# Column tiles for the values of two more pairs of head groups, and other ranks for four streams of a planned kernel

## The chip, the cores and the metric

The kernel runs on one core of a Trainium2 chip. The metric is the device time of one execution in microseconds. A core has a matmul engine (PE, with its weight loads listed as PEld), a vector engine (DVE), a scalar engine (ACT), GpSimd (POOL) and SyncE (SP), whose queue issues nearly all DMAs here.

## The reference

Two layers over a sequence of 2048 tokens of width 640, each an attention block and a feed-forward block, with layer norm ahead of each and a residual sum behind it. All weights are shared by the two layers.

```python
for layer in range(2):
    x = x + attention(layernorm(x), wq, wk, wv, wo, beta)
    h = layernorm(x)
    x = x + max(h @ w1, 0) @ w2            # w1: 640 x 1728

# attention: 32 heads of 20, four segments of 512 tokens; g = sigmoid(beta), per head
for s in range(4):
    p = softmax(q_s k_s^T / sqrt(20), causal inside the segment)
    a_dot = p v_s
    a_mem = phi(q_s) M / (phi(q_s) z + 1e-6)   # phi(t) = t + 1 if t > 0 else exp(t)
    o_s = g * a_mem + (1 - g) * a_dot
    M, z = M + phi(k_s)^T v_s, z + sum phi(k_s)
return concat(o) @ wo
```

## The kernel before

The program is not written as loops. Every piece of the work is a Python generator, called a stream, which yields operations (an engine, an assumed duration, the instructions, what they wait for) and requests for buffers and events. A planner, `Sched.run`, takes one operation after the other and so writes out each engine's order of instructions ahead of time. It picks the operation that can start first by its own reckoning; among those that start at the same nanosecond, the lower rank wins. The rank is the first argument of `S.add(rank, stream)` at the end of `plan`. Streams of rank 0, the score products and the exponentials, may also keep an engine from starting something that would delay them.

```python
key = (round(start + late), op.urgent * 0.5 if op.urgent else prio, n)
```

The kernel makes a whole plan for each value in `STARTS`, which is the price in ns that the planner puts on a change of PE's tile mode, and keeps the plan that comes out shortest by its own reckoning with random lateness of DMAs (`late`). PE works in three modes: `full` (the 128 x 128 array), `rows` (four row tiles, for the scores, whose contraction is a head of 20) and `cols` (column tiles). An operation in column mode that is ready while PE is in full mode is held up to 4 us (`JOIN_NS`), so that it can follow a round of scores. Where the planner sees no work for PE it puts in idle matmuls on a unit matrix (`keep_busy`, line 627).

A segment's 32 heads are 8 groups of 4, taken as 4 pairs; `m` counts the pairs over both layers, 0 to 31, and pairs 0 to 3 are the first segment of the first layer. For each pair the steps are:

- `fill` brings q and k of the pair's heads into a padded buffer, by DMA from a scratch area in HBM that `spill` has written.
- `scores` (line 1103) and `exps` (L1155) run in five rounds over two halves of PSUM; `causal` (L1167) masks on POOL.
- `apply` multiplies the probabilities by the values. There are two forms. In the first segment of the first layer, `values_by_token` (L1197) has the probabilities stationary and 21 value columns moving, so that tokens come out on the partitions; DVE divides straight from PSUM (L1209 to L1213). Everywhere else the values are stationary in four column tiles (L1246); the result is copied out of PSUM (L1254 on DVE or L1255 on ACT), `turn_av` transposes it by a DMA through SP's queue, and `divide` (L1282 to L1290) divides it on DVE.
- `combine` adds the memory's part, `turn_o` transposes o by DMA, `out_proj` multiplies by wo and adds to x (L1317).

`phi_(0)` and `phi_(1)` compute phi of k and of q (L956 and L964 on DVE, L963 on ACT), `turn_k` transposes phi(k) by DMA, `mem_write` (L1047 to L1068) updates the memory and `mem_read(0)` and `mem_read(1)` (L996 to L1007) read it for one half of the heads each. `ffn` is the feed-forward; `ffn_last` (L1394) computes the last 64 of its 1728 hidden columns in two column tiles and is a stream of its own, whose result `ffn` waits for.

The planner streams run through all 8 pairs of layer and segment in order. Full-array products of the projections, of `out_proj` and of `ffn` come from one helper, with the first product of a group on line 640 and the others on line 643; all DMA transposes are issued on line 671.

Of the kernel before, what the change touches and what calls it, by code (L numbers as in the profile page):

```python
# [14 lines left out]
NSEG = 4  # L15
# [4 lines left out]
G = H // 4  # L20
# [137 lines left out]

LONE_NS = 300.0
SWITCH_NS = 97.0  # L160
STARTS = [SWITCH_NS + 0.75 * (k - 32 // 2) for k in range(32)]
LATE_NS = 300.0
JOIN_NS = 4000.0
SEM_NS = 60.0
# [212 lines left out]
def pe(ns, fns, waits=(), acq=None, take=(), mode="full"):  # L377
    return Op([("pe", ns, fns, 190.0)], waits, acq=acq, take=take, mode=mode)
# [6 lines left out]
def dve(n, mode, fn, waits=(), extra=0.0, acq=None, urgent=False):  # L385
    return Op([("dve", 66.0 + n / (0.96 * mode) + extra, [(fn, True)], 95.0)], waits, acq=acq, urgent=urgent)


def act(n, fn, waits=(), psum=True):
    return Op([("act", (52.0 if psum else 94.0) + n / 1.2, [(fn, True)], 125.0)], waits)  # L390
# [17 lines left out]
def plan(switch, sb, sem_, psum, dram, A_x, A_wq, A_wk, A_wv, A_wo, A_beta, B_x, B_w1, B_w2, out):  # L408
    P = Prog({e: sem_("clk_" + e) for e in ["act", "dve", "pool", "pe"]})
    S = Sched(P, switch)  # L410
# [437 lines left out]
    def sx(a, s):  # L848
        return 1 if (a, s) == (0, 1) else 0
# [92 lines left out]
    def phi_(n):  # L942
        def f(a, s):
            if s == (NSEG - 1, 0)[n]:
                for c in range(FC):
                    p = yield Need("packed", a, s, c)
                    STG[sx(a, s)][n][c].release(*p)
                return
            done = []
            for c in range(FC):  # L950
                if n == 0 and c in (0, 3):
                    yield Acq([PHS[c // 3]])
                raw = yield Need("stg", a, s, c, n)
                q = STGS[sx(a, s)][:, c, n, :]
                rt = yield Acq(RT)
                tr = yield dve(512, 4, lambda e, rt=rt, q=q: e.tensor_scalar(  # L956
                    rt.ap, q, 0.0, 1.0, ALU.max, ALU.add), raw + rt.tks)
                if n == 0:
                    dst, w = phs[:, c * L:(c + 1) * L], raw + PHS[c // 3].tks
                else:  # L960
                    p = yield Need("packed", a, s, c)
                    dst, w = q, [tr] + p
                te = yield act(512, lambda e, q=q, dst=dst: e.activation(dst, q, ACT.Exp), w, psum=False)  # L963
                tp = yield dve(512, 2, lambda e, rt=rt, dst=dst: e.tensor_tensor(dst, dst, rt.ap, ALU.min),  # L964
                               [te, tr])
                rt.release(tp)
                done.append(tp)
                if n == 0:
                    p = yield Need("packed", a, s, c)
                    STG[sx(a, s)][0][c].release(te, tr, *p)  # L970
                    if sx(a, s):
                        early_done.extend([te, tr] + p)
                    if c in (2, 4):
                        S.set("phk", a, s, c // 3, tks=done)
                        done = []
            if n == 1:
                S.set("phi", a, s, tks=done)
        return f
# [4 lines left out]
    def mem_read(hb):  # L983
        def f(a, s):
            if s == 0:
                return
            phi = yield Need("phi", a, s)
            bdt = yield Need("BD", a, s - 1)
            yield Acq([OMS[hb]])
            wr = []  # L990
            lst = [(c, max(CH_H0[c], 16 * hb), min(CH_H1[c], 16 * hb + 16)) for c in range(FC)]
            lst = [x for x in lst if x[1] < x[2]]
            for i in range(NJ):
                fns = []
                for z, (c, h0, h1) in enumerate(lst):
                    fns.append((lambda e, bk, c=c, h0=h0, h1=h1, z=z, i=i: e.matmul(  # L996
                        bk.ap[:, (h0 - 16 * hb) * 21:(h1 - 16 * hb) * 21],
                        STGS[sx(a, s)][:, c, 1, i * 128:(i + 1) * 128],
                        BD[:, CH_OFF[c] + (h0 - CH_H0[c]) * 21:CH_OFF[c] + (h1 - CH_H0[c]) * 21],
                        start=(z == 0), stop=True, skip_group_check=True), z == len(lst) - 1))  # L1000
                bk, tk = yield pe(60.0 * len(lst), fns, phi + bdt, acq=MISC[:1])
                rm = yield Acq(RMEM[hb])
                om = bk.ap[:, 0:336].rearrange("p (h e) -> p h e", e=21)
                ta = yield dve(16, 1, lambda e, rm=rm, om=om: e.tensor_scalar(
                    rm.ap, om[:, :, DH:DH + 1], 1e-6, None, ALU.add), [tk] + rm.tks)
                tr = yield dve(96, 1, lambda e, rm=rm: e.reciprocal(rm.ap, rm.ap), [ta])
                tm = yield dve(320, 1, lambda e, rm=rm, om=om, i=i: e.tensor_tensor(  # L1007
                    om_sb[:, i, 320 * hb:320 * hb + 320].rearrange("p (h e) -> p h e", e=DH),
                    om[:, :, 0:DH], rm.ap.to_broadcast([128, 16, DH]), ALU.mult), [tr] + OMS[hb].tks)
                rm.release(tm)  # L1010
                bk.release(tm)
                wr.append(tm)
            S.set("omem", a, s, hb, tks=wr)
            READ.setdefault((a, s), []).append(tk)
            if len(READ[a, s]) == 2:
                for c in range(FC):
                    STG[sx(a, s)][1][c].release(*READ[a, s])
                if sx(a, s):
                    S.set("q01", tks=READ[a, s])
                BDS.release(*READ[a, s])  # L1020
        return f
# [154 lines left out]

        return 32 if (g, hh) != (G - 1, 3) else DH + 1

    BY_TOKEN = ((0, 0),)

    def values_by_token(m, a, s, g0, vt):

# [37 lines left out]
    def done_values(a, s, g0, tk):  # L1220
        if g0 == G - 2:
            dmt = yield Need("dm", a, s)
            VA[vx(a, s)].release(tk, *dmt)
            if (a, s) == (0, 0):
                S.set("v00", tks=VA[3].tks)

    def apply(m):

        a, r = divmod(2 * m, NSEG * G)
        s, g0 = divmod(r, G)  # L1230
        vt = yield Need("v", a, s)
        if (a, s) in BY_TOKEN:
            tk = yield from values_by_token(m, a, s, g0, vt)
            yield from done_values(a, s, g0, tk)
            return
        sl = None
        ev = []
        for z in range(2):
            mk = yield Need("p", 2 * m + z)
            pt, mk = mk[0], mk[1:]  # L1240
            if sl is None:
                sl = yield Acq([AV])
            fns = []
            for j in range(NJ):
                for hh in range(4):
                    fns.append((lambda e, bk, j=j, hh=hh, pt=pt, g=g0 + z: e.matmul(  # L1246
                        bk.ap[32 * hh:32 * hh + wide(g, hh), 128 * j:L],
                        VAUG[vx(a, s)][:, j].rearrange("p h e -> p (h e)")[
                            :, (4 * g + hh) * (DH + 1):(4 * g + hh) * (DH + 1) + wide(g, hh)],
                        pt.ap[:, hh, PT_OFF[j]:PT_OFF[j] + L - 128 * j], start=(j == 0), stop=(j == NJ - 1)),  # L1250
                        j == NJ - 1 and hh == 3))
            bk, tk = yield pe(545.0, fns, mk + vt, acq=MISC, mode="cols")
            pt.release(tk)
            te = yield evac(L, 1, lambda e, sl=sl, z=z, bk=bk: e.tensor_copy(sl.ap[:, z], bk.ap),  # L1254
                            lambda e, sl=sl, z=z, bk=bk: e.activation(sl.ap[:, z], bk.ap, ACT.Copy), [tk] + sl.tks)  # L1255
            bk.release(te)
            ev.append(te)
        S.set("av", m, tks=[sl] + ev)
        yield from done_values(a, s, g0, tk)

    LATER = range(len(BY_TOKEN) * G // 2, NSEG * G)

    def turn_av(m):
        ev = yield Need("av", m)
# [207 lines left out]
    def each(f):  # L1472
        for a, s in AS:
            yield from f(a, s)
# [8 lines left out]
    S.add(1, items(apply, NSEG * G))  # L1483
    S.add(2, items(turn_av, LATER))
    S.add(6, items(divide, LATER))
    S.add(2, each(hot(turn_o)))
# [5 lines left out]
    S.add(5.5, each(spill))  # L1492
    S.add(2, each(combine))
    S.add(4, each(phi_(0)))
    S.add(4, each(phi_(1)))
    S.add(4, each(mem_read(0)))
    S.add(1, each(mem_read(1)))
    S.add(4, each(turn_k))
    S.add(4, each(mem_write))
    S.add(5, first_ln_a())  # L1500
    S.add(5, first_ln_b())
# [3 lines left out]
    S.add(5, each(proj_one(1)))  # L1505
    S.add(4, each(proj_v))
    S.add(6, each(ffn))
    S.add(6, each(ffn_last))
    S.add(7, warm_pe())
    S.add(3, consts())  # L1510
    S.add(8, loads())
# [6 lines left out]
def bass_interleave_layers__memory_aug_infini_attn__dense_activation_relu__prompt_kernel(  # L1518
    nc, A_x, A_wq, A_wk, A_wv, A_wo, A_beta, B_x, B_w1, B_w2, out,
):  # L1520
    with contextlib.ExitStack() as es:
# [10 lines left out]
        dram = lambda name, shape: once(name, lambda: nc.dram_tensor(name, shape, dt.bfloat16, kind="Internal").ap())  # L1532
        plans = [plan(k, sb, sem_, psum, dram, A_x, A_wq, A_wk, A_wv, A_wo, A_beta, B_x, B_w1, B_w2, out) for k in STARTS]
        S = min(plans, key=lambda p: sum(p.late(n) for n in range(4)))
# [31 lines left out]
```

## Time and profile before

| | |
|---|---|
| median of 3 runs | 566.28 us (564.82 to 566.39) |
| the profiled execution | 565.3 us, of which 563.5 are the span of instructions |
| PE, DVE, ACT, POOL busy | 99%, 75%, 72%, 35% of the span |
| L1197, values by token | 320 matmuls |
| L1246, values by column tiles | 896 matmuls |
| L627, idle matmuls | 66 |
| L1394, ffn_last | 80 matmuls |
| DMA, mean share of the 16 engines | 45.5% on the main queue |

The span is counted from the first to the last instruction; the profiled execution's own time has 1.8 us around it. In lists of groups a row gives line, engine, operation, output and inputs, the count, busy time and mean duration in ns, and then idle time of the engine before these instructions and what ended it. In timelines a row is start, length, engine, line and what is done, with the number of instructions merged. Matmuls overlap in the pipeline, so the distance between two starts is the time that one takes from PE's queue, and not its duration.

### The profile page before, as it was taken

What the parts mean: (1) busy time and instruction counts of PE and PEld (TensorE: products, weight loads), DVE (VectorE), ACT (ScalarE), POOL (GpSimd) and SP (SyncE); (2) the same over time, 40 slices, a digit from 0 to 9 for tenths busy, and PEclk for the clock granted to TensorE, in tenths of its full rate; (3) what the DMA queues carried; (4) which work ended last, traced back from release to release, by engine and by line L of the source; (5) the groups of instructions that cost most, each with busy time, mean ns of one, the idle gap of its engine ahead of it and who ended that gap; (6) DMA issues with size and microseconds to landing.
All of it is one profiled execution on the core that took longest, in us unless ns stands there. A gap on an engine that the chain in (4) does not pass through costs nothing.

```text
span 563.5 us, 12875 instructions
## 1 busy us (share of the span) xinstructions
PE 556.4 (99%) x5219; PEld 305.0 (54%) x5219; DVE 420.1 (75%) x1070; ACT 404.2 (72%) x512; POOL 195.1 (35%) x302
## 2 busy tenths in 40 slices
PE   8999999999999999999999999999999999999998
PEld 7664555445554454645446544555445654665655
DVE  6989789888999689878898997688747964560202
ACT  4789998987788878778986688778878678113140
POOL 4544344333344335444433443035322433110000
PEclk9999999999999999999999999999999999999999
DMA  8695988383474136542375131880326410512101
GB/s 268 120 221 138 238 218 182 74 224 56 97 171 94 44 88 159 118 95 72 92 163 115 27 66 26 193 148 20 67 80 173 109 43 20 116 45 48 47 1 47
DMA packets 130109, 60.93 MB, mean 108 GB/s; under 512 B 108930, under 2 KB 119938, under 8 KB 130050
## 3 DMA queue, kind: packets, MB, share of 16 engines
q1 hardware_dynamic: 129830, 59.85, 45.5%
q8 instruction: 41, 0.67, 0.5%
q10 hardware_dynamic: 220, 0.26, 0.2%
q14 instruction: 18, 0.15, 0.1%
HBM read 20.57 MB, written 12.85 MB: 59 GB/s over the span
## 4 chain that ended last, share of the span: by engine, by line
PE 87%; DVE 8%; DMA 2%; ACT 1%; SPq 1%; issue 0%
PE ps L643 56%; PE ps L640 11%; PE ps L1103 8%; PE ps L1246 6%; DVE stats L651 2%; PE ps L996 2%; PE ps L1197 1%; PE ps L1047 1%; DVE x_sb L1317 1%; PE ps L1394 1%; DMA avt<-av 1%; DVE xn_tok L705 1%; SPq L913 1%; DMA oT<-o_sb 1%; ACT PT L1155 1%; DVE stg L816 1%
## 5 line engine op out<-in xcount | busy, mean ns | idle before, releaser
L1155 ACT ACTIVATE PT<-ps 128x1024 bf16<-128x1024 f32 x320 | 310.0, 1022 | 70.3 <-PE ps L1103 64.6
L1167 POOL TENSOR_SCALAR_AFFINE_SELECT PT<-PT 128x512 bf16<-128x512 bf16 x256 | 166.6, 668 | 268.2 <-ACT PT L1155 267.9
L643 PE MATMUL ps<-w_r,hT 128*128 128x320 bf16 (+2 forms) x768 | 123.0, 299 | 0.0
L643 PE MATMUL ps<-xnT,w_r 128*128 128x512 bf16 x416 | 113.3, 379 | 0.0
L1317 DVE TENSOR_TENSOR x_sb<-x_sb,ps 128x320 bf16<-128x320 bf16 (+1 forms) x128 | 60.3, 479 | 66.7 <-PE ps L643 66.0
L643 PEld LDWEIGHTS ps<-w_r,hT 128*128 128x128 bf16 x768 | 72.4, 98 | 31.9 <-issue 4.4
L1425 ACT ACTIVATE hT<-ps 128x512 bf16<-128x512 f32 x55 | 32.7, 598 | 50.0 <-PE ps L643 49.7
L1103 PE MATMUL ps<-pad 20*128 20x128 bf16 (+3 forms) x1024 | 64.8, 301 | 1.6 <-ACT PT L1155 0.9
L643 PEld LDWEIGHTS ps<-xnT,w_r 128*128 128x128 bf16 x416 | 39.7, 98 | 44.0 <-issue 3.2
L651 DVE BATCH_NORM_STATS2 stats<-x_sb 128x6 f32<-128x320 bf16 x126 | 56.4, 472 | 2.1 <-DMA x_sb<-in_A_x_dram 1.8
L1254 DVE CAST av<-ps 128x512 bf16<-128x512 f32 x53 | 36.2, 684 | 14.8 <-PE ps L1246 14.7
L1103 PEld LDWEIGHTS ps<-pad 20*128 20x128 bf16 x1024 | 18.3, 92 | 52.6 <-ACT PT L1155 25.6
L643 PE MATMUL ps<-wo_r,oT 128*128 128x320 bf16 x256 | 46.1, 299 | 0.0
L1246 PE MATMUL ps<-PT,v_aug 128*32 128x256 bf16 (+5 forms) x896 | 40.7, 302 | 0.0
L1423 DVE TENSOR_SCALAR hT<-ps 128x512 bf16<-128x512 f32 x49 | 33.4, 683 | 9.1 <-PE ps L643 9.0
L640 PE MATMUL ps<-xnT,w_r 128*128 128x512 bf16 x104 | 39.6, 380 | 0.0
L643 PE MATMUL ps<-wv_r,xnT 128*128 128x320 bf16 x192 | 36.7, 300 | 0.0
L643 PE MATMUL ps<-xnT,wk_r 128*128 128x512 bf16 (+1 forms) x140 | 36.1, 349 | 0.0
L643 PE MATMUL ps<-xnT,wq_r 128*128 128x512 bf16 (+1 forms) x140 | 34.9, 349 | 0.0
L665 POOL TENSOR_TENSOR rstd<-lnU,mhalf 128x2 f32<-128x2 f32 (+2 forms) x25 | 20.8, 831 | 38.0 <-DVE lnU L661 34.4
L816 DVE CAST stg<-ps 128x512 bf16<-128x512 f32 (+1 forms) x48 | 29.5, 618 | 3.3 <-PE ps L643 3.2
L1290 DVE TENSOR_TENSOR o_sb<-avt,rden 128x320 bf16<-128x320 bf16 x56 | 30.5, 562 | 0.6
(117 smaller groups left out, 695.8 us busy)
## 6 DMA issues: line engine op xcount, KB each, us to landing
pad<-scr SPq DMA_DIRECT2D x124, 80.0 KB
scr<-stg SPq DMA_DIRECT2D x34, 256.0 KB, 2.9
out_dram<-x_sb SPq DMA_DIRECT2D x15, 160.0 KB, 1.8
w_r<-in_B_w_dram SPq DMA_DIRECT2D x10, 216.0 KB, 4.2
w_r<-in_B_w_dram SPq DMA_DIRECT2D x13, 160.0 KB, 2.8
x_sb<-in_A_x_dram SPq DMA_DIRECT2D x9, 160.0 KB, 2.8
scr<-w_r SPq DMA_DIRECT2D x5, 256.0 KB, 3.6
x_sb<-in_A_x_dram SPq DMA_DIRECT2D x3, 320.0 KB, 7.2
```

The costliest lines, as they stand in the source:

```text
L640: bk, tk = yield pe(mm_ns(n), [(lambda e, bk, a=a, b=b: e.matmul(bk.ap[:, 0:n] if len(b.shape) == 2 else bk.ap[:, 0:n].rearrange("p (i n) ...
L643: tk = yield pe(mm_ns(n), [(lambda e, k=k, a=a, b=b, bk=bk: e.matmul(bk.ap[:, 0:n] if len(b.shape) == 2 else bk.ap[:, 0:n].rearrange("p (i ...
L651: tk = yield dve(320, 1, lambda e, c2=c2: e.bn_stats(stats6[:, t, c2, :], x_sb[:, t, c2 * 320:(c2 + 1) * 320]), xt)
L816: te = yield evac(N, 1, lambda e, sg=sg, bk=bk: e.tensor_copy(sg.ap[:, t0:t0 + N], bk.ap[:, 0:N]), lambda e, sg=sg, bk=bk: e.activation(sg ...
L1103: fns.append([(lambda e, z=z, j=j, hh=hh, N=N, o=o, sl=sl: e.matmul(ps[:, hh, o:o + N], sl.ap[32 * hh:32 * hh + DH, z, 0, 128 * j:128 * j ...
L1155: tx = yield act(1024, lambda e, dst=dst, src=src: e.activation(dst, src, ACT.Exp, scale=SCALE), sc + pw)
L1167: tm = yield pool(600.0, lambda e, reg=reg: e.affine_select(out=reg, in_=reg, pattern=[[0, 4], [1, 128]], compare_op=ALU.is_ge, fill=0.0, ...
L1246: fns.append((lambda e, bk, j=j, hh=hh, pt=pt, g=g0 + z: e.matmul(bk.ap[32 * hh:32 * hh + wide(g, hh), 128 * j:L], VAUG[vx(a, s)][:, j].re ...
L1254: te = yield evac(L, 1, lambda e, sl=sl, z=z, bk=bk: e.tensor_copy(sl.ap[:, z], bk.ap), lambda e, sl=sl, z=z, bk=bk: e.activation(sl.ap[:, ...
L1317: ta = yield dve(n, 1, lambda e: e.tensor_tensor(x_sb[:, t, c0:c0 + n], x_sb[:, t, c0:c0 + n], bk.ap[:, 0:n], ALU.add), [tk] + list(waits) ...
L1423: th = yield evac(512, 1, lambda e, dc=dc, bk=bk: e.tensor_scalar(hT[:, dc, :], bk.ap[:, :], 0.0, None, ALU.max), lambda e, dc=dc, bk=bk: ...
L1425: lambda e, dc=dc, bk=bk: e.activation(hT[:, dc, :], bk.ap[:, :], ACT.Relu), [tk] + HT.tks)
```

## The change

Six edits. `STARTS` has 48 values instead of 32, with the same step around the same middle. The choice of the form of the values goes by pair and not by layer and segment: pairs 2 and 3 stay with `values_by_token`, pairs 0 and 1 go to column tiles, copy, DMA transpose and `divide`; `LATER`, the list of pairs for `turn_av` and `divide`, follows. Four streams get other ranks: `phi_(1)` 6.5 instead of 4, `mem_read(0)` 4.5 instead of 4, `turn_k` 6.5 instead of 4, `ffn_last` 2.5 instead of 6.

```diff
-STARTS = [SWITCH_NS + 0.75 * (k - 32 // 2) for k in range(32)]
+STARTS = [SWITCH_NS + 0.75 * (k - 48 // 2) for k in range(48)]
...
-    BY_TOKEN = ((0, 0),)
+    BY_TOKEN = (2,3)
...
-        if (a, s) in BY_TOKEN:
+        if m in BY_TOKEN:
             tk = yield from values_by_token(m, a, s, g0, vt)
             yield from done_values(a, s, g0, tk)
             return
...
-    LATER = range(len(BY_TOKEN) * G // 2, NSEG * G)
+    LATER = [m for m in range(NSEG * G) if m not in BY_TOKEN]
...
     S.add(4, each(phi_(0)))
-    S.add(4, each(phi_(1)))
-    S.add(4, each(mem_read(0)))
+    S.add(6.5, each(phi_(1)))
+    S.add(4.5, each(mem_read(0)))
     S.add(1, each(mem_read(1)))
-    S.add(4, each(turn_k))
+    S.add(6.5, each(turn_k))
     S.add(4, each(mem_write))
...
     S.add(6, each(ffn))
-    S.add(6, each(ffn_last))
+    S.add(2.5, each(ffn_last))
```

## The prediction

> **What bounds the kernel now.** I read the page first: busy shares, and the span in 40 slices.
>
> ```profile
> PE 556.4 (99%) x5219; PEld 305.0 (54%) x5219; DVE 420.1 (75%) x1070; ACT 404.2 (72%) x512; POOL 195.1 (35%) x302
> ...
> PE   8999999999999999999999999999999999999998
> ```
>
> The matmul engine (PE) is busy for 556.4 of 563.5 us, in every slice but the first and the last. So its queue sets the end, and a microsecond counts only if it leaves that queue, either as a matmul, as a change of tile mode, or as a hole. This page does not separate those three. The timeline of PE does, read by the distance from one start to the next.
>
> ```profile
> 107.81 0.38 PE L640 MATMUL ps<-xnT,wk_r 128*128 128x512 bf16 x1
> 108.13 0.40 PE L1103 MATMUL ps<-pad 20*128 20x512 bf16 x4
> 108.45 0.34 PE L996 MATMUL ps<-BD,w_r 128*128 128x147 bf16 x3
> 108.64 1.02 PE L643 MATMUL ps<-xnT,wk_r 128*128 128x512 bf16 x4
> 109.50 0.59 PE L643 MATMUL ps<-xnT,w_r 128*128 128x512 bf16 x2
> 110.02 0.74 PE L1394 MATMUL ps<-xnT,w_r 128*64 128x256 bf16 x10
> 110.69 0.40 PE L1103 MATMUL ps<-pad 20*128 20x384 bf16 x8
> 111.02 0.73 PE L1246 MATMUL ps<-PT,v_aug 128*32 128x512 bf16 x16
> 111.68 0.34 PE L996 MATMUL ps<-BD,w_r 128*128 128x147 bf16 x3
> ```
>
> Full-array matmuls of 512 columns follow each other at (109.50 - 108.64)/4 = 0.215 us. The same matmul ahead of the score products of L1103, which use row tiles, takes 108.13 - 107.81 = 0.32, so a change of tile mode costs about 0.10 us. The value products of L1246 (16 matmuls in column tiles, one group of four heads) take 111.68 - 111.02 = 0.66 us with the change that follows. They stand directly behind a round of scores. The last block of the feed-forward's hidden layer, L1394, is in column tiles too and takes 110.69 - 110.02 = 0.67 us, but here it comes out of full mode and runs ahead of the scores, so it pays a change of its own.
>
> The other form of the value products, L1197, is used for the first segment alone: 40 small full-mode matmuls a group.
>
> ```profile
> 70.35 1.18 PE L1197 MATMUL ps<-w_r,PT 128*128 128x21 bf16 x40
> 71.38 1.02 PE L643 MATMUL ps<-hT,wk_r 128*128 128x512 bf16 x4
> ```
>
> That is 71.38 - 70.35 = 1.03 us a group, with no change of mode after it.
>
> Then I read the windows of 5 us for the place where PE is not full of real work (columns: length, then busy time of PE, PEld, DVE, ACT and POOL, each with a count; then the granted clock, which is 1.00 throughout).
>
> ```profile
> core 0: us, PE busy (x) PEld busy (x) DVE busy (x) ACT busy (x) POOL busy (x), PEclk, DMA share, GB/s
> 60.00:65.00 5.00, 5.00 (x82) 3.35 (x81) 3.26 (x9) 4.92 (x9) 1.85 (x3) 1.00 1.01 256
> 65.00:70.00 5.00, 5.00 (x32) 2.28 (x29) 3.70 (x9) 4.53 (x6) 2.44 (x4) 1.00 1.17 226
> 80.00:85.00 5.00, 4.79 (x69) 3.07 (x69) 3.16 (x8) 4.98 (x7) 2.08 (x4) 1.00 1.19 213
> 90.00:95.00 5.00, 4.73 (x48) 2.27 (x46) 5.00 (x16) 3.28 (x5) 2.04 (x4) 1.00 0.68 233
> 95.00:100.00 5.00, 4.54 (x48) 2.03 (x46) 4.96 (x16) 4.99 (x8) 3.00 (x5) 1.00 0.72 159
> ```
>
> PE lacks 0.21, 0.27 and 0.46 us in three of these windows, 0.94 together. DVE, the vector engine, is full from 90 to 100 and had 1.74 and 1.30 us free between 60 and 70. The 80 to 85 window hides more: idle-matmuls (L627) that the planner puts where it has nothing for PE.
>
> ```profile
> 80.34 1.40 PE L627 MATMUL ps<-ident 128*128 128x128 bf16 x22
> 81.68 0.39 PE L1103 MATMUL ps<-pad 20*128 20x512 bf16 x2
> 82.00 0.51 PE L627 MATMUL ps<-ident 128*128 128x128 bf16 x6
> ...
> 84.00 0.31 PE L640 MATMUL ps<-wo_r,oT 128*128 128x320 bf16 x1 [0.21 <-DMA oT<-o_sb]
> ```
>
> 1.40 + 0.51 = 1.9 us of filler, until the transposed attention output oT of the first segment lands at 84.00. With the 0.94, some 2.8 us between 80 and 100 are holes. Outside this stretch I see no hole worth a term.
>
> **The change part by part.** The planner reorders everything behind an edit, so each term has two ends.
>
> *(a) Values of pairs 0 and 1 of the first segment by column tiles.* Four groups (two pairs of two) leave L1197 for L1246. Joined to a round of scores, each saves 1.03 - 0.66 = 0.37 us; four save 1.5. If none joins, each pays one more change, 0.27 each, 1.1 together. These groups lie before 60 us, and whether the saving arrives depends on the hole at 80: if the landing of oT doesn't move, PE only waits longer there, and the saving is 0. The landing hangs on the value products of pair 3, which stay in the old form and wait for that pair's exponentials, not for PE. Against that, PE reaches the projections earlier, and with them the work that feeds the hole. Between 0 and -1.5 I take the middle, -0.8, since nothing in the rows is near to either end.
>
> What (a) adds: per pair two evacuations, one reciprocal, two products on DVE, in place of two reciprocals and two products from PSUM, and a DMA transpose.
>
> ```profile
> L1254 DVE CAST av<-ps 128x512 bf16<-128x512 f32 x53 | 36.2, 684 | 14.8 <-PE ps L1246 14.7
> ...
> L1290 DVE TENSOR_TENSOR o_sb<-avt,rden 128x320 bf16<-128x320 bf16 x56 | 30.5, 562 | 0.6
> ...
> L1213 DVE TENSOR_TENSOR o_sb<-ps,rden 128x320 bf16<-128x320 f32 x8 | 3.9, 485 | 0.1
> ```
>
> 2 x 0.684 + 2 x 0.545 = 2.5 us (L1290 as busy time over count, 30.5/56) against 2 x 0.485 = 1.0 us: 1.5 us more DVE time a pair, 3.0 for both. That is an upper end: of reciprocals and gate products, left out here, the column form has one a pair and the old form two. I cost it at nothing because the 1.74 + 1.30 = 3.0 us that DVE has free from 60 to 70 cover it, and because the two divisions are needed only by the time pair 3 is done. Without that cover it costs what the second rival says. The transposes:
>
> ```profile
> avt<-av SPq DMA_TRANSPOSE x28, 2.8
> ```
>
> 28 become 30, 2.8 us from issue to landing. They go on SP's queue, past pad fills, spills, loads of weights and the transposes of phi(k); these wait behind them for about one issue each. The price is between 0 and, if a pad comes late and the scores wait for it, two landings (5.6 us) of attention time, which PE would fill with projections. I take 0.
>
> *(b) ffn_last from rank 6 to 2.5.* Behind value products PE is in column mode already, and at 2.5 this stream now goes ahead of projections and feed-forward there, where it had lost to both. It saves the change of its own.
>
> ```profile
> busy tenths in 40 slices 0000000200002000020000020002000020020200
> ```
>
> Eight executions, in slices of 14.1 us: six before 465 us, two after 490.
>
> ```profile
> L1255 ACT ACTIVATE av<-ps x3: 597/597/597, 356.3 to 483.5; 128x512 bf16<-128x512 f32 x3
> ```
>
> The last evacuations of values are at 483.5, so the last two have nothing to join. For six, the saving is 0 to 2 changes each (none where values follow directly, two where it stands alone in full mode), 0 to 1.2 us; at one, as in the row at 110.02, six make -0.6.
>
> *(c) phi_(1) and turn_k from 4 to 6.5, mem_read(0) from 4 to 4.5.* A rank decides only among instructions that could start at the same time, so mostly on the engine with a backlog, DVE. From 85 to 100 the chain of waits runs through DVE, and there it has
>
> ```profile
> 86.33 0.34 DVE stg L964
> 86.67 0.64 DVE rtmp L956
> ```
>
> between residual adds that the layer norm and the feed-forward of the first segment wait for. The L964 row is phi of the queries, of which nobody is in need for that moment, as memory read of a later segment. At 6.5 such work steps behind the adds, and what depends on it, the memory products (L996) and the combination, comes later. On SP, phi(k)'s transpose stood ahead of oT:
>
> ```profile
> 77.35 2.71 SPq L671 DMA_TRANSPOSE phk<-phs  x1
> 80.10 3.16 SPq L671 DMA_TRANSPOSE oT<-o_sb  x2
> ```
>
> and o_sb, which oT reads, was complete at about 79.1:
>
> ```profile
> 78.66 0.48 DVE L1213 TENSOR_TENSOR o_sb<-ps,rden 128x320 bf16<-128x320 f32 x1
> ```
>
> so oT was issued about 1.0 us after its data. Rank does not cure this by itself, as at 77.35 oT was not ready. Bounds: gain of all holes, 2.8; nothing; or a loss as in the third rival. I take the 0.94 us of idle as recovered and leave the filler: -0.9.
>
> *(d) 48 starting values instead of 32.* It tries more values of the assumed price of a mode change and keeps the plan that it reckons shortest. The first 32 were 85 to 108.25 ns, the new ones 79 to 114.25, around the 0.10 us measured above. Nothing by itself; the plan is another one, and I take 0 between -1 and +1 (ten changes of mode either way).
>
> Sum: -0.8 - 0.6 - 0.9 = -2.3 us against the profiled execution, 565.3 us, of which 563.5 is the span: 563.0. The median of the runs, 566.28, is 1.0 above the profiled execution, so I predict 564.0.
>
> **The rivals.** First, *nothing to measure*: the hole at 80 swallows all of (a) and the ranks find no tie to break; (b) stays, -0.6: 565.7. For it speaks that the filler stands there at all; against it, the DVE rows at 86. What a measurement here can tell from no change is about 0.3%, 1.7 us. Chance 0.17.
>
> Second, *slower by DVE*. The 3.0 us more fall behind 70 us and not into the free time between 60 and 70, because the division has rank 6 and is served last. Then the last o_sb, oT's landing and the end of the hole come up to 3.0 later; PE has nothing else there, so all of it counts, and (a) is lost. With (b): +3.0 - 0.6 = +2.4, 568.7. It decides where the divisions of pairs 0 and 1 stand: before about 70 us it costs nothing. For it speaks that DVE is full at 90 to 100; against it the free 3.0 us. The Trainium skill (TensorEngine Tiling (Array Packing), PSUM Bottleneck) states this as a rule: tiling speeds up the matmul but not the copy out of PSUM, which may become the limit. By that rule (a) is a loss here; the evacuation rows agree that the copies are there, and no row of before shows what they delay. Chance 0.16.
>
> Third, *slower by late memory reads*. At 6.5, phi of the queries is pushed back again and again, the memory products come last in a segment, and the combination and oT wait for them: a hole like that at 80 to 85 in further segments. One is worth 1.9 + 0.21 = 2.1 us; two of them against the sum of (a) and (b), -1.4, give +2.8: 569.1. It decides when the last memory product of a segment comes after the last division of its values. Against it: the second half, mem_read(1), keeps rank 1, and PE had other work at every other segment end. Chance 0.12.
>
> That ranks or tiles don't do what they say I count in the first rival: the pairs in column tiles are certain from the code.
>
> **How the numbers follow.** The forecast, faster by over 0.3% (below 564.6), has 0.55; its own range is from all upper ends, -1.5 - 1.2 - 2.8 = -5.5 (560.8), to 564.6. The first rival is the "same" case, 0.17. The second and third make slower, 0.28. The range for 8 in 10 leaves out the top of the third rival and the last bit of the upper ends: 561.0 to 569.0.
>
> **What would show it.** L1197 with 160 matmuls instead of 320 and L1246 with 960; avt transposes 30; PE's busy time down by about 1.4; L1394 directly behind L1246 in about six places. At 80 to 85 us: filler no more than 1.9 us and oT landing no later than 84 says that (a) arrived; filler of 3 us or more says that it was swallowed. The windows from 90 to 100 show PE full if (c) works. I am wrong if DVE's divisions of pairs 0 and 1 stand behind 70 us with oT late, if PE shows holes at later segment ends, or if the new plan has many more changes of mode, 0.10 us each.

## The result

The changed kernel takes 573.79 us in the median (572.13 to 575.57, four runs) against 566.07; the ratio is 1.0141, with an interval of 1.0106 to 1.0176. It is slower by 1.4%, where the prediction had 564.0 us and a range up to 569.0.

The page of the changed kernel, the same lines as before:

```profile
PE 557.3 (97%) x5110; PEld 302.5 (53%) x5111; DVE 422.2 (74%) x1080; ACT 401.3 (70%) x502; POOL 195.1 (34%) x302
...
PE   8999999998999999999999999999999999999998
...
PEclk9999998999999999999999999999999999999999
```

The profiled execution takes 574.27 us, with a span of 572.5. PE is busy for 0.9 us more than before (557.3 against 556.4) and idle for 572.5 - 557.3 = 15.2 us, against 563.5 - 556.4 = 7.1. So of the 9.0 us of span, 8.1 are waits of PE. They are spread: the slice at 129 to 143 us shows them as an 8, and the longest is 1.84 us. The clock has an 8 at 86 to 100 us.

The windows that the prediction looked at, with 40 to 60 ahead of them:

```profile
core 0: us, PE busy (x) PEld busy (x) DVE busy (x) ACT busy (x) POOL busy (x), PEclk, DMA share, GB/s
40.00:60.00 20.00, 18.63 (x196) 9.08 (x195) 19.71 (x51) 17.09 (x22) 8.73 (x13) 1.00 0.67 167
60.00:65.00 5.00, 5.00 (x72) 2.86 (x70) 4.97 (x16) 4.58 (x7) 2.05 (x3) 1.00 0.99 236
65.00:70.00 5.00, 3.58 (x36) 2.21 (x35) 2.52 (x9) 3.42 (x5) 1.22 (x2) 1.00 1.05 213
80.00:85.00 5.00, 5.00 (x42) 1.95 (x34) 4.67 (x18) 4.69 (x6) 2.11 (x4) 1.00 0.62 171
90.00:95.00 5.00, 5.00 (x39) 2.74 (x38) 3.97 (x12) 2.81 (x4) 1.00 (x2) 0.83 1.04 195
95.00:100.00 5.00, 5.00 (x51) 2.88 (x50) 5.00 (x17) 4.28 (x7) 1.92 (x3) 1.00 0.41 99
```

and the same first window of the kernel before:

```profile
40.00:60.00 20.00, 20.00 (x243) 10.18 (x242) 19.93 (x54) 18.32 (x24) 8.68 (x13) 1.00 0.63 154
```

Before, PE was full in all these windows up to 80. Now it lacks 1.37 us between 40 and 60 and 1.42 between 65 and 70. The 1.42 us are one hole, in which the products that update the memory (L1047) wait for the transposed phi(k):

```profile
69.00 0.97 PE L1047 MATMUL ps<-v_aug,phk 128*128 128x147 bf16 x12 [1.42 <-DMA phk<-phs]
```

From 80 on the windows look full, but 90 to 95 has a clock of 0.83, and in between lies this:

```profile
86.05 0.73 PE L1246 MATMUL ps<-PT,v_aug 128*32 128x512 bf16 x16 [0.84 <-POOL PT L1167]
86.71 0.40 PE L1103 MATMUL ps<-pad 20*128 20x384 bf16 x8
87.91 0.34 PE L996 MATMUL ps<-BD,w_r 128*128 128x84 bf16 x3 [0.80 <-DVE om_sb L1007]
...
89.26 0.47 PE L640 MATMUL ps<-wo_r,oT 128*128 128x320 bf16 x1
89.52 0.47 PE L643 MATMUL ps<-wo_r,oT 128*128 128x320 bf16 x1
89.79 0.47 PE L640 MATMUL ps<-wo_r,oT 128*128 128x320 bf16 x1
...
93.77 0.30 PE L640 MATMUL ps<-wo_r,oT 128*128 128x320 bf16 x1
93.90 0.30 PE L643 MATMUL ps<-wo_r,oT 128*128 128x320 bf16 x1
```

Two holes, 0.84 and 0.80 us. The rows name what each waits for: first a mask on POOL (L1167), then a product of DVE (L1007). Behind them the products of 320 columns follow each other at 0.26 us (89.26, 89.52, 89.79), and later at 0.13 (93.77, 93.90).

```profile
86.00:88.00 2.00, 1.15 (x26) 0.56 (x27) 2.00 (x6) 1.95 (x3) 1.28 (x2) 1.00 1.09 315
88.00:90.00 2.00, 2.00 (x11) 1.22 (x12) 1.91 (x7) 1.60 (x3) 0.85 (x2) 0.56 1.02 282
90.00:92.00 2.00, 2.00 (x11) 0.86 (x9) 1.35 (x5) 0.00 (x0) 0.37 (x1) 0.58 0.91 192
```

The granted clock is about a half for 3.4 us, which costs some 1.7 us ((1 - 0.56) x 2 + (1 - 0.58) x 2). The Trainium skill (TensorE: Matmul & The Clock Gate, HAM oscillation) sums this up as a rule against idle gaps of PE above about 3.4 us. No gap here is that long, and the clock fell all the same, so the trace decides. The half clock follows two of 0.8 us with 1.1 us of work between them (86.05 to 87.11), while no half clock follows the longer holes of 1.42 us at 69 and 1.84 us at 131. So the length of one gap doesn't tell here when the clock falls. The mean clock isn't the same in each run: of the four runs of the changed kernel the three with a mean clock of 0.997 took 573.31 to 575.57, the one at 1.0 took 572.13.

The longest hole is at 131:

```profile
130.92 0.40 PE L1103 MATMUL ps<-pad 20*128 20x384 bf16 x8
133.16 0.73 PE L1246 MATMUL ps<-PT,v_aug 128*32 128x512 bf16 x16 [1.84 <-DVE hT L1423]
```

PE waits 1.84 us for an evacuation (L1423) that frees the bank it needs. The evacuation isn't late by its own doing. It stands in DVE's queue behind a division:

```profile
127.25 0.49 DVE L1007 TENSOR_TENSOR om_sb<-ps,rmem 128x320 bf16<-128x320 f32 x1
131.22 0.35 DVE L1282 RECIPROCAL rden<-avt 128x32 f32<-128x32 bf16 x1 [3.48 <-DMA avt<-av]
131.61 0.19 DVE L1283 TENSOR_TENSOR rden<-rden,omg 128x32 f32<-128x32 f32 x1
131.84 0.49 DVE L1290 TENSOR_TENSOR o_sb<-avt,rden 128x320 bf16<-128x320 bf16 x1
132.25 0.17 DVE L1004 TENSOR_SCALAR rmem<-ps 128x16 f32<-128x16 f32 x1
132.33 0.68 DVE L1423 TENSOR_SCALAR hT<-ps 128x512 bf16<-128x512 f32 x1
```

DVE stood still for 3.48 us until the transpose of avt had landed, 6.5 us after its issue, and the evacuation at 132.33 had to stand in line behind it. The Trainium skill (TensorE: Matmul & The Clock Gate, Architectural detail) says that DVE serves its queue strictly in order. The trace agrees: DVE runs nothing until 131.22, though PE had ended its last whole group of hidden products ahead of the hole by 129.10 + 1.03 = 130.13 us. And the transpose was issued behind loads of w2:

```profile
122.42 1.30 SPq L532 DMA_DIRECT2D w_r<-in_B_w_dram  x3
124.10 0.56 SPq L544 DMA_DIRECT2D w_r<-in_B_w_dram  x1
124.71 1.31 SPq L671 DMA_TRANSPOSE avt<-av  x1
```

### The profile page after: what moved, and what is told of

It reads as the page before. It is cut to its first block, busy times and chain, and to the rows that moved or that the text cites. A ratio compares the mean times of both kernels' runs of the same rounds, so it can differ in the third digit from the quotient of the medians.

```text
span 572.5 us, 12665 instructions
## 1 busy us (share of the span) xinstructions
PE 557.3 (97%) x5110; PEld 302.5 (53%) x5111; DVE 422.2 (74%) x1080; ACT 401.3 (70%) x502; POOL 195.1 (34%) x302
## 4 chain that ended last, share of the span: by engine, by line
PE 63%; DVE 24%; DMA 7%; ACT 2%; issue 1%; SPq 1%; POOL 1%; ACTq 0%
PE ps L643 41%; PE ps L640 8%; PE ps L1103 5%; PE ps L1246 5%; DVE stats L651 4%; DMA avt<-av 3%; DVE x_sb L1317 2%; DVE av L1254 2%; DVE o_sb L1290 2%; DVE stg L816 2%; DVE xn_tok L693 1%; DMA phk<-phs 1%; PE ps L996 1%; ACT PT L1155 1%; DVE xn_tok L705 1%
## 5 line engine op out<-in xcount | busy, mean ns | idle before, releaser
L1167 POOL TENSOR_SCALAR_AFFINE_SELECT PT<-PT 128x512 bf16<-128x512 bf16 x256 | 166.3, 667 | 275.7 <-ACT PT L1155 275.5
L643 PE MATMUL ps<-w_r,hT 128*128 128x320 bf16 (+2 forms) x768 | 124.8, 299 | 0.1
L1317 DVE TENSOR_TENSOR x_sb<-x_sb,ps 128x320 bf16<-128x320 bf16 (+1 forms) x128 | 60.1, 478 | 63.7 <-PE ps L643 63.3
L1103 PE MATMUL ps<-pad 20*128 20x384 bf16 (+3 forms) x1024 | 64.5, 301 | 1.7 <-DMA pad<-stg 0.6
L1254 DVE CAST av<-ps 128x512 bf16<-128x512 f32 x57 | 38.9, 683 | 18.4 <-PE ps L1246 18.2
L1425 ACT ACTIVATE hT<-ps 128x512 bf16<-128x512 f32 x58 | 34.8, 599 | 19.9 <-PE ps L643 19.5
L643 PE MATMUL ps<-wo_r,oT 128*128 128x320 bf16 x256 | 47.9, 307 | 0.0
L1246 PE MATMUL ps<-PT,v_aug 128*32 128x256 bf16 (+5 forms) x896 | 40.7, 302 | 2.9 <-DVE hT L1423 1.8
L1423 DVE TENSOR_SCALAR hT<-ps 128x512 bf16<-128x512 f32 x46 | 31.5, 684 | 10.6 <-PE ps L643 10.4
L816 DVE CAST stg<-ps 128x512 bf16<-128x512 f32 (+1 forms) x51 | 31.6, 624 | 5.9 <-PE ps L643 5.8
L1290 DVE TENSOR_TENSOR o_sb<-avt,rden 128x320 bf16<-128x320 bf16 x60 | 32.4, 555 | 0.7
```

What stands on the lines that cost most here:

```text
L643: tk = yield pe(mm_ns(n), [(lambda e, k=k, a=a, b=b, bk=bk: e.matmul(bk.ap[:, 0:n] if len(b.shape) == 2 else bk.ap[:, 0:n].rearrange("p (i ...
L816: te = yield evac(N, 1, lambda e, sg=sg, bk=bk: e.tensor_copy(sg.ap[:, t0:t0 + N], bk.ap[:, 0:N]), lambda e, sg=sg, bk=bk: e.activation(sg ...
L1103: fns.append([(lambda e, z=z, j=j, hh=hh, N=N, o=o, sl=sl: e.matmul(ps[:, hh, o:o + N], sl.ap[32 * hh:32 * hh + DH, z, 0, 128 * j:128 * j ...
L1167: tm = yield pool(600.0, lambda e, reg=reg: e.affine_select(out=reg, in_=reg, pattern=[[0, 4], [1, 128]], compare_op=ALU.is_ge, fill=0.0, ...
L1290: to = yield dve(320, 1, lambda e, dst=dst, src=src, rz=rz: e.tensor_tensor(dst, src, rz, ALU.mult), [tg] + OSB.tks)
L1317: ta = yield dve(n, 1, lambda e: e.tensor_tensor(x_sb[:, t, c0:c0 + n], x_sb[:, t, c0:c0 + n], bk.ap[:, 0:n], ALU.add), [tk] + list(waits) ...
```

## The experiments

In the diffs below, "old" values are those of the kernel before. Ratios are against runs of the kernel before taken next to each kernel, so they are not quotients of the medians in the table; behind them stands the interval; idle is span minus PE's busy time in the profiled execution.

| kernel | edits of the change in it | price of a mode change, ns | median us | ratio | PE idle us |
|---|---|---|---|---|---|
| before | none | 85.75 | 566.07 | 1 | 7.1 |
| changed | all | 105.25 | 573.79 | 1.0141 (1.0106 to 1.0176) | 15.2 |
| both_81 | all | 81.25 | 567.74 | 1.0009 (0.9988 to 1.0030) | 9.7 |
| both_97 | all | 97.0 | 566.53 | 1.0008 (0.9986 to 1.0031) | 7.3 |
| both_80 | all | 80.5 | 566.84 | 1.0014 (0.9993 to 1.0036) | 8.4 |
| both_99 | all | 99.25 | 568.68 | 1.0027 (1.0009 to 1.0045) | 9.6 |
| both_84 | all | 84.25 | 569.83 | 1.0064 (1.0038 to 1.0089) | 9.8 |
| tok_89 | column tiles | 89.5 | 570.94 | 1.0078 (1.0050 to 1.0106) | 11.3 |
| ranks_79 | ranks | 79.0 | 568.32 | 1.0016 (0.9997 to 1.0036) | 10.0 |
| old_108 | none | 108.25 | 569.19 | 1.0058 (1.0031 to 1.0086) | 10.1 |
| old_85 | none | 85.0 | 567.69 | 1.0035 (1.0014 to 1.0056) | 8.0 |
| old_82 | none | 82.75 | 568.47 | 1.0033 (1.0018 to 1.0048) | 6.7 |
| old_48 | 48 starting values | 114.25 | 570.89 | 1.0086 (1.0058 to 1.0114) | 10.9 |
| after_w2_behind | all, four loads moved | 105.25 | 569.95 | 1.0072 (1.0047 to 1.0097) | 12.2 |
| both_fix | all, longer reckoning | 81.25 | 565.38 | 0.9978 (0.9966 to 0.9990) | 5.8 |
| both_lat3 | all, longer landing | 83.5 | 569.97 | 1.0060 (1.0045 to 1.0075) | 8.1 |
| both_dve | all, longer DVE steps | 88.0 | 568.65 | 1.0044 (1.0023 to 1.0064) | 9.2 |
| old_fix | none, longer reckoning | 97.75 | 570.33 | 1.0068 (1.0044 to 1.0092) | 10.5 |
| tok_fix | column tiles, longer reckoning | 88.75 | 568.06 | 1.0032 (1.0016 to 1.0048) | 6.7 |
| ranks_fix | ranks, longer reckoning | 100.0 | 568.32 | 1.0038 (1.0023 to 1.0053) | 7.8 |

### The edits, or the one plan?

Four kernels separate the edits from the plan that was picked. Each keeps the streams and changes ranks, tiles or the price with which the plan is made.

```diff
 # both_81
-STARTS = [SWITCH_NS + 0.75 * (k - 48 // 2) for k in range(48)]
+STARTS = [81.25]
 # old_108: STARTS = [108.25], and the old ranks and
-    BY_TOKEN = (2,3)
+    BY_TOKEN = (0, 1, 2, 3)
 # tok_89: STARTS = [89.5] and the old ranks;  ranks_79: STARTS = [79.0] and BY_TOKEN = (0, 1, 2, 3)
```

> All edits of the change, but a plan made with one starting value only, 81.25 ns for a change of tile mode in place of the 105.25 that the changed kernel chose for itself. Theory P (the plan): the edits are sound, and the time was lost because a plan that overprices mode changes (0.10 us measured) lets PE arrive before the DVE and DMA results that it expects; with 81.25 the other engines come early, and the holes of PE go back to about those of before: 562 to 567 us. Theory T (tiles) and theory R (ranks) hold that an edit itself makes the holes in any plan: 570 to 576 us.

> None of the edits to ranks and tiles; the plan of before made with 108.25 ns in place of its own choice of 85.75. Theory P: like the changed kernel it overprices mode changes, PE's holes grow by several us and the time is 571 to 578. Theories T and R: without the edits there is nothing that holds PE up beyond what the order costs, 564 to 569.

> Column tiles for pairs 0 and 1 alone, ranks as before; the planner's own choice among the 48 starting values, which is 89.5. Theory P: the price is below the measured one, so 562 to 567. Theory T: the copies and divisions of two more pairs lie on DVE while it is full (19.9 of 20 us busy from 40 to 60 before), PE gets holes before 100 us, 569 to 574. Theory R: nothing is wrong here, 564 to 566.

> The four other ranks alone, all four first pairs by token as before; the planner's own choice among the 48 starting values, 79.0. Theory P: 560 to 566, holes as in before. Theory T: as before or a little faster, 563 to 566. Theory R: the late transposes of phi(k) and late phi of q hold PE up as in the changed kernel (1.42 us at 67.6 us there), 569 to 574.

With all edits and another price the time is that of before, 1.0009; 567.74 us lies 0.7 above the range of theory P and under that of the two others. So tiles and ranks don't cost 1.4% whatever the plan. Theory P, that an overpriced mode change is to blame, is not right in this form either: old_108 is slower, but by 0.58%, under the range it gave. And the tiles alone, at a price under the measured one, are slower by 0.78%. That is inside the range of theory T, and the kernel has a hole of 1.44 us at 57; but both_81 has the same tiles and no such wait there. ranks_79, with 568.32 us, fits none of the three ranges. What is left is that the plan matters as much as the edits.

### One cause in the changed plan: a transpose behind loads

The changed kernel's own plan, all queues as they were, but SP issues the last four loads of w2 after the transpose of avt.

```diff
         S = min(plans, key=lambda p: sum(p.late(n) for n in range(4)))
+        sp = S.P.ops["sp"]                 # the plan's order of SP's queue
+        ...                                # take out the four loads of w2 ahead of the transpose
+        sp[t - 3:t - 3] = items            # and put them behind it
```

> The changed kernel with its own plan (105.25), every engine's order as it was, but on SP's queue the last four loads of w2 go behind the transpose of avt that they preceded (it took 6.5 us from issue to landing at 124.7, DVE waited 3.48 us for it and PE had its longest hole, 1.84 us, behind an evacuation in DVE's queue). Theory L (late landings): the holes are transposes that land later than the plan reckons, because other transfers are in flight, and DVE serves its queue in order; the avt transpose lands in 3 to 4.5 us, the hole at 131 shrinks to under 0.7 and the time falls by 1 to 2 us to 571.5 to 573. Theory O (the order itself is too tight at many places): the hole only moves on, 573 to 574.5.

```profile
121.46 1.24 SPq L671 DMA_TRANSPOSE avt<-av  x1
122.75 2.92 SPq L532 DMA_DIRECT2D w_r<-in_B_w_dram  x3
125.71 0.56 SPq L544 DMA_DIRECT2D w_r<-in_B_w_dram  x1
...
126.17 0.35 DVE L1282 RECIPROCAL rden<-avt 128x32 f32<-128x32 bf16 x1 [1.48 <-DMA avt<-av]
...
127.28 0.68 DVE L1423 TENSOR_SCALAR hT<-ps 128x512 bf16<-128x512 f32 x1
```

The transpose is issued ahead of the loads and lands 126.17 - 121.46 = 4.7 us later, a little over the 3 to 4.5 expected. DVE waits 1.48 us in place of 3.48, the evacuation of hT follows at 127.28, and PE loses nothing:

```profile
128.00:134.00 6.00, 6.00 (x67) 2.88 (x63) 3.21 (x7) 4.64 (x6) 2.03 (x4) 1.00 0.19 57
```

against the same stretch of the changed kernel:

```profile
128.00:134.00 6.00, 4.16 (x44) 1.81 (x43) 2.71 (x9) 4.62 (x6) 2.33 (x5) 1.00 0.57 91
```

The median falls from 573.79 to 569.95, the ratio from 1.0141 to 1.0072. That is more than the 1.84 us of the hole, and below the 571.5 to 573 of theory L. This kernel's profiled execution has no stretch at half clock, and three of its four runs were at a clock of 1.0 (569.82 to 569.96), the fourth at 0.997 with 572.06. At the same clock of 1.0 the two kernels stand at 572.13 (one run) and 569.9: 2.2 us, about the hole. The holes of 0.84 and 0.80 us are still there, ending at 84.41 and 86.28, so why the clock stayed up more often isn't shown.

The two profiles differ by 572.5 - 568.1 = 4.4 us, and most of it is not the move's. PE's order is the same in both kernels, and these are the same matmuls, just ahead of the transpose, in the changed kernel and in this one:

```profile
123.79 0.81 PE L643 MATMUL ps<-xnT,w_r 128*128 128x512 bf16 x3
...
120.74 0.81 PE L643 MATMUL ps<-xnT,w_r 128*128 128x512 bf16 x3
```

So 3.05 us arise ahead of them, where nothing waits for the loads that were moved: the half clock, and the hole of 1.42 us at 69, which this execution doesn't have. Both come in one execution of an order and not in another. That a late transpose behind loads makes the hole at 131 is shown here; the other holes were not tried one by one.

### A plan that reckons with the measured steps

In the trace of the changed kernel, five small DVE steps take longer than the planner reckons, the gate product and the reciprocal of a division above all, and some transposes land late. These kernels give the planner longer figures and let it plan and choose anew.

```diff
 # lat: in turn()
-                       issue=max(1400.0, 140.0 * n), lat=2000.0, rate=270.0, holds=True)
+                       issue=max(1400.0, 140.0 * n), lat=3000.0, rate=270.0, holds=True)
 # dve: in divide(), mem_read() and stats()
-        tr = yield dve(192, 1, lambda e: e.reciprocal(...), tT + rd.tks)
+        tr = yield dve(192, 1, lambda e: e.reciprocal(...), tT + rd.tks, extra=108.0)
 # the gate product extra=128.0, reciprocal and sum of mem_read 63.0 and 35.0, bn_aggr 41.0
 # both_fix: lat and dve;  both_lat3: lat;  both_dve: dve;  old_fix, tok_fix, ranks_fix: lat and dve
```

> All edits; the planner reckons with what the trace of the changed kernel shows: five small DVE steps longer (the gate product of a division 227 ns from start to start where it reckoned 99, its reciprocal 374 for 266, three others by 35 to 63), and a DMA transpose landing 1 us later. It plans anew and chooses 81.25. Theory L: holes of PE fall to those of before or less, 561 to 566. Theory O (any plan with these edits is a draw between 565 and 574): 566 to 571.

> All edits; the planner reckons 1 us more for the landing of a transpose and nothing else; it chooses 83.5. Theory L: most of the gain, 562 to 567. Theory O: 566 to 571. If this is much slower than the kernel that also has the DVE steps, DVE's chain counts more than the landings.

> All edits, the planner reckons with the longer DVE steps alone, transposes as before; it chooses 88.0. With 1 us more for transposes alone it measured 570.0, with both 565.4. If the DVE steps are what the plan lacked: 564 to 567. If it takes both, or if each plan is a draw: 567 to 572.

> None of the edits to ranks and tiles; the planner reckons with the longer DVE steps and 1 us more for a transpose, as in the kernel with all edits that measured 565.4. It chooses 97.75 ns. Theory E (the edits are worth nothing net, the plan decides): 564 to 567.5, within 0.3% of that kernel. Theory S (the sum of the prediction, tiles and ffn_last save some 1.4 to 2 us of PE's queue): 567 to 569.

> Column tiles for pairs 0 and 1, old ranks, the same longer reckoning; it chooses 88.75. Theory E: 564 to 568, with idle-matmuls or a hole of 1.3 us or more between 40 and 64 us, where the saved PE time ends. Theory S: about 1 us under the kernel without edits and no hole there.

> The four ranks alone, the same longer reckoning; it chooses 100.0. Theory E: 564 to 568, about as the kernel without edits, no idle-matmuls between 40 and 64. Theory S: 0.6 to 1.5 us under the kernel without edits, from ffn_last behind the values and from less waiting between 85 and 100.

both_fix is the fastest kernel of the study, 0.22% under before, with the least idle time of PE (5.8 us). But this isn't the effect of the longer figures alone: either half of them gives 1.0060 and 1.0044, and without the edits they give 1.0068. Theory L, that the longer landing is most of the gain, missed with both_lat3 (562 to 567 expected, 570 measured). Under the same longer figures the edits look worth 0.9% (old_fix against both_fix), tiles and ranks alone 0.36% and 0.30%. That is the direction of theory S, but old_fix, with 570.33 us, is above the ranges of both theories, and tok_fix and ranks_fix, with 568.06 and 568.32, are just above that of theory E. Under the planner's old figures the same comparison, before against changed, goes the other way. One plan for each is too few to read an edit's worth from.

Nor does the wait for late avt transposes set the time of a plan by itself. This row stands under who waited for avt in the changed kernel (us, times):

```profile
  DVE rden L1282: 10.4, 8
```

The same row reads 6.7 in 5 places before and 1.6 in 2 in both_81; in both_fix it is absent. But old_fix has 0.7 and is at 1.0068, slower than before with its 6.7. At 131 us the wait cost time because PE came to need the evacuation behind it.

### More draws

```diff
 # both_97, both_80, both_99, both_84: all edits;  old_85, old_82: none
-STARTS = [SWITCH_NS + 0.75 * (k - 48 // 2) for k in range(48)]
+STARTS = [97.0]          # 80.5, 99.25, 84.25;  85.0, 82.75
 # old_48: old ranks, BY_TOKEN = (0, 1, 2, 3), STARTS as in the changed kernel
```

> All edits, nothing else changed, planned with 97 ns as price of a mode change, about the price measured. It is a second draw beside the plan with 81.25, which measured 567.7. If the loss of the changed kernel belongs to its one plan, this is 565 to 570; if the edits lose at prices near the measured one, 571 to 576.

> The edit of STARTS alone: old ranks, all four first pairs by token, 48 values; the planner then chooses 114.25, a value that the 32 did not have. Theory E (each plan is a draw): 564 to 573, as likely above 567.5 as below. If the prediction's reading of this edit is right, within 1 us of before.

> No edit but one value, 85.0, the neighbour of the 85.75 of before. Theory E: neighbouring prices give unrelated plans, 565 to 571. If the price itself matters: within 1 us of before, 565 to 567.

> All edits, 80.5 ns. Theory E: 563 to 571. Theory that the edits cost something: 568 to 574.

> All edits, 99.25 ns. Theory E: 563 to 571. Theory that the edits cost something: 568 to 574.

> No edit but one value, 82.75 ns. Theory E (each plan is a draw): 565 to 571.

> All edits, 84.25 ns. Theory E: 563 to 571. Theory that the edits cost something: 568 to 574.

Six plans with all edits, the changed kernel's own among them, and the planner's old figures: 0.08% to 1.41% over before, 0.44% in the mean. Four further plans without the edits to ranks and tiles: 0.33%, 0.35%, 0.58% and 0.86% over, 0.53% in the mean. A price 0.75 ns away from that of before gives 0.35% more. So these plans show no cost of the edits on average; the kernel before holds the best plan of its kind that was run, and the changed kernel holds the worst of all. Whether the edits are worth a few tenths of a per cent by themselves stays open: the plans of one kind differ by more.

## Why the prediction was wrong

**The step that failed is (d), the plan.** I wrote that "the plan is another one" and took 0 between -1 and +1 us for it, from ten changes of mode either way. Changes of mode hardly moved: 395 in the changed kernel against 393, counted over PE's matmuls by line. What moves there are the waits. In other plans it is PE's busy time: old_82 is idle for less than before (6.7 against 7.1 us) and still 0.33% over, with 93 idle matmuls in place of 66 and 401 changes of mode, and both_lat3 has 123 idle matmuls. So the idle time in the table doesn't rank the plans by itself. The plans that were run lie from 0.22% under before to 1.41% over, some 1.2 us to 8.0, so the term was mis-sized by a factor of several, and it was larger than the sum of all others.

The edit of `STARTS` alone, old_48, is 0.86% slower, where I wrote "nothing by itself". The planner reckons that plan shorter than the one of before, which is among its 48, so its reckoning does not rank them by time. In the changed kernel that edit did nothing, since 105.25 is also one of the 32 old values.

**(a), column tiles.** The PE side came as forecast: 160 of the small matmuls are left, and 64 are new.

```profile
L1197 PE MATMUL ps<-w_r,PT 128*128 128x21 bf16 x160 | 4.8, 172 | 0.0
...
L1246 PE MATMUL ps<-PT,w_r 128*32 128x512 bf16 (+3 forms) x64 | 2.9, 302 | 0.0
```

From start to start, L1197 takes 4.29 us of PE's queue in all where it took 8.30, and L1246 takes 39.60 where it took 36.96: 1.4 us less together, near the 1.5 of the joined case. But the saving didn't arrive in the time. I placed the hole that might swallow it at 80 us; it opened at 54 instead, where PE now runs ahead of the layer norm of the third segment:

```profile
54.83 0.89 PE L627 MATMUL ps<-ident 128*128 128x128 bf16 x13
...
57.06 0.31 PE L640 MATMUL ps<-wv_r,hT 128*128 128x320 bf16 x1 [1.03 <-DMA hT<-xn_tok]
```

That is 0.89 us of filler and 1.03 us of waiting for the transposed norm, 1.9 us against a saving of 1.5. All plans with the column tiles that were run have idle matmuls between 52 and 62 us (13 to 64 of them), and of the kernels without them neither before nor old_82, old_85, old_108, old_48 or old_fix has one there. But ranks_fix has 22, and ranks_79 has its longest hole there, 2.57 us at 62.23, for the same transposed norm, so the ranks alone can do it too. So the first rival's mechanism is what happens to (a), at another place. DVE is the likely reason, not one that a run isolates: it is 19.93 of 20 us busy from 40 to 60 before, and there the new copies fall. I had looked for cover in the free time from 60 to 70, behind the point where they land. This is half of the second rival; its place isn't: the divisions of pairs 0 and 1 start between 45.6 and 63.3 us, ahead of 70, and no idle matmul is left from 70 to 100.

**(b), ffn_last.** The order came as forecast in three of the six places:

```profile
109.00 0.40 PE L1103 MATMUL ps<-pad 20*128 20x384 bf16 x8
109.32 0.73 PE L1246 MATMUL ps<-PT,v_aug 128*32 128x512 bf16 x16
109.98 0.74 PE L1394 MATMUL ps<-xnT,w_r 128*64 128x256 bf16 x10
110.65 0.39 PE L643 MATMUL ps<-xnT,wk_r 128*128 128x512 bf16 x1
```

But no change of mode is saved by it, and this step of the prediction failed too. L1246 takes 109.98 - 109.32 = 0.66 us with L1394 behind it, as it does with a product in full mode behind it (111.02 to 111.68 in the prediction's rows). L1394 takes 110.65 - 109.98 = 0.67, as it did when it came out of full mode. The other way round it is the same. Before, two of the six places already had the two directly behind each other:

```profile
170.50 0.74 PE L1394 MATMUL ps<-xnT,w_r 128*64 128x256 bf16 x10
171.17 0.73 PE L1246 MATMUL ps<-PT,v_aug 128*32 128x512 bf16 x16
171.83 0.34 PE L1103 MATMUL ps<-pad 20*128 20x384 bf16 x4
```

So as far as these distances show, L1246 with four column tiles of 32 and L1394 with two of 64 share no mode that saves a change: behind the values the stream adds one change, as it did ahead of the scores at 110.02. Counted so, the six executions add seven changes before and seven now, and the -0.6 is 0.

**(c), ranks.** I took the idle time between 80 and 100 as recovered. The three windows that lacked 0.94 us are full, but two new holes at 85 to 88 make 1.64 us. ranks_79 and ranks_fix, 0.16% and 0.38% over before, show no gain either. The hole of 1.42 us at 69 is a wait for `turn_k`, which the edit moved to 6.5. Yet PE waits so for phi(k) in old_108 and old_48 as well (1.7 and 1.1 us in all), with the old ranks, and in no other plan with the new ones but after_w2_behind (0.3), so the rank isn't shown to be its cause.

**The rivals.** The third was right that slower means holes in several places, but its cause, late memory reads, ends one hole of those shown, 0.80 us. The longest comes from a transpose that stands behind weight loads. The prediction priced only the reverse, what the two new transposes do to the transfers behind them, at 0; this one, issued at 124.71, is not one of the two (41.8 and 56.6). What I had not seen is that a division waiting in DVE's queue holds up the evacuations behind it, and with them PE's banks.

PE's busy time was to fall by 1.4 us and rose by 0.9. The half clock adds 1.7; column tiles and 12 idle matmuls fewer take off some 2.5 together. The remaining 1.7 us or so were not traced to a cause. So the account is whole for the hole at 131, and for the other waits it goes as far as what they wait for.

## What to carry to other kernels

Where a planner writes out the whole order, a small edit is a new draw, and its worth can't be read from one plan: run several plans of each side and compare the groups. Ask of a transfer that moves onto a queue not only who waits for it, but what stands behind the waiter in its in-order queue; moving four loads behind one transpose took away the longest hole, some 2 us of this loss. Longer figures for steps that the plan reckons too short are no cure by themselves: of the six plans made with them one was faster than before.

## What was not expected of the hardware

The DMA transposes of avt in the changed kernel, all of one size, took 2.7 us from issue to landing at the least, 2.9 in the median and 6.5 at the most, the last with four pad fills and four weight loads directly ahead of it on the queue (119.93 to 124.66). PE's clock fell to about a half for 3.4 us after two holes of 0.8 us each; after_w2_behind has the same two holes and no fall. In ranks_79 the clock is 0.50 from 64 to 66 us, after the hole of 2.57. The run of after_w2_behind with a mean clock of 0.997 took 572.06 us, the three at 1.0 took 569.82 to 569.96.
